# The last pair of down projections of a block moves behind the next block's output projection

## The chip, the cores and the metric

The kernel runs on one core of one Trainium2 chip. The metric is the device time of one execution in microseconds. The engines named below are TensorE (PE, with its weight loads as PEld), VectorE (DVE), ScalarE (ACT), GpSimd (POOL) and SyncE (SP, which issues the DMA transfers).

## The reference

One transformer layer on 2048 tokens of width 512. Attention has 32 heads of 16 with a single key and value head; the feed-forward part is a gated bilinear unit of width 1792. Shifts, scales and gates come from a condition vector.

```python
mod = (silu(c) @ w_mod).reshape(c.shape[0], 6, 1, -1)
sa, ca, ga, sb, cb, gb = (mod[:, i] for i in range(6))
h = layernorm(x) * (1 + ca) + sa
q = (h @ wq)             # 32 heads of 16
k, v = h @ wk, h @ wv    # one head of 16
p = softmax((q @ k.T) * 16 ** -0.5)
x = x + ga * ((p @ v) @ wo)
h = layernorm(x) * (1 + cb) + sb
x = x + gb * (((h @ w_gate) * (h @ w_up)) @ w_down)
```

## The kernel before, in words

The 2048 tokens are cut into 4 blocks of 512. Attention of a block is 8 **units** of 4 heads each, so there are 32 units, 0 to 31; a unit is 32 **steps**, and the loop has 1024 of them. A step computes, two times over, 512 columns of scores for the running maximum of the next unit (tile `mx`, reduced by DVE into `mpart`), 512 columns of scores (tile `sc`, exponentiated by ACT into tile `P`) and 512 columns of the product with the values (tile `pv`). So a step has two exponentials on ACT and two maximum reductions on DVE.

All other matmuls are **fill**: the planner puts them between these, at the end of a step. Fill consists of groups, each the sum over a long contraction into one PSUM bank (tile `misc`; the bank is `misc` or `spare`): the query projections (16 groups of 12 terms, in units 0 to 7), and then for each block the output projection (`wo_work`, 4 groups of 12), the gate and up projections (`ffn_work`, 28 groups of 12) and the down projections (4 groups of 42). Operands are split into high and low halves in fp16, which gives three terms per product.

A term of a group is computed as two **halves**, one on the upper 64 rows of PE and one on the lower 64. Two groups run side by side: one on rows 0 to 63, the other on rows 64 to 127; together that is a **pair** of halves, eight PE instructions of 64x32 by 512 columns. A group starts on the upper half beside the lower half of its predecessor, which is called the carry. A stretch of such pairs that ends with an eviction is a **turn** (`begin_turn`, `end_turn`); a turn of gate or up groups has 12 pairs. The first group of a chain has no predecessor and the last no successor, so at both ends 12 halves run alone. Down projections come as `twos`: two groups that take 12, 30 and 42 pairs.

The queue `fill` is in an order written out by hand at step 16 of the first unit of a block: the 4 output projections of the block just finished, the transposes of the second normalisation (`ln2_work`, "solo" items, four, one for each 128 columns), the 28 gate and up groups, the two pairs of down projections. Each item has a due step. `pace` works out from the due steps how many pairs a step has to take, and `fill_gap` issues up to `BURST` = 3 pairs per step from the credit so gained. A turn starts `EV_WAIT` = 1 step after one that ended with an eviction, else `SWAP_WAIT` = 2. The transposes wait `TR_GAP` = 8 steps after the output projection, for its sums (`x1`), their statistics on DVE and POOL and the normalised rows `n2` on ACT. A transposed piece goes through ACT (`hf`, two buffers) and is split by POOL into the two halves of `h2T`. While block 0 is treated, POOL also still splits the feed-forward weights (tile `wsl` into `wg` and `wu`), one slice every two or three steps, in an order that does not depend on the fill.

The sums `x1` of a block live from its output projection to the end of its down projections, in a ring of 4 buffers that `hi` and `gab` of the start share. Block 3 has no attention after it: its work, and what is left of block 2, runs in a tail of plain 128x128 matmuls. The two pairs of down projections of block 2 are left to that tail.

Of the kernel before, what the change touches and what calls it, by code (L numbers as in the profile page):

```python
# [13 lines left out]
F32 = mybir.dt.float32  # L14
F16 = mybir.dt.float16
# [4 lines left out]
S, D, H, DH, F = 2048, 512, 32, 16, 1792  # L20
KC = D // 128
NB = 4
BT = S // NB
# [15 lines left out]
SWAP_WAIT = 2  # L39
EV_WAIT = 1  # L40
TURN = 12
RESERVE = 31000.0
TR_GAP = 8
BURST = 3
# [11 lines left out]
def adaln_mqa_glu_kernel(ctx: ExitStack, tc: tile.TileContext, x_in, wq_in, wk_in, wv_in, wo_in,  # L56
# [7 lines left out]
    work = ctx.enter_context(tc.tile_pool(name="work", bufs=2))  # L64
# [23 lines left out]
    def ps_misc(shape=(128, 512), dt=F32, tag=None):  # L88
        bufs = 1
        if tag is None:  # L90
            tag, bufs = ring["tags"][ring["n"] % len(ring["tags"])]
            ring["n"] += 1
        elif tag == "sc":
            bufs = NSC
        return psum.tile(list(shape), dt, name="misc", tag=tag, bufs=bufs)
# [102 lines left out]
    def rstd_of(st, n):  # L198
        y = work.tile([128, 4], F32, name="ry", bufs=6)[:, :n]
        rstd_into(y, st[:, :, 1], n)  # L200
        return y
# [59 lines left out]
                             start=(k == 0), stop=(k == KC - 1))  # L261

    def split_rows(dst, p, scale, mscale, bias):
        hi = work.tile([128, BT], F16, name="hi", tag="x1", bufs=4)
        nc.scalar.activation(hi, p, AF.Identity, bias=bias, scale=mscale)
        nc.vector.scalar_tensor_tensor(dst, p, scale, hi, op0=OP.mult, op1=OP.subtract)

# [396 lines left out]
    def after(delay, f):  # L664
        if tick[0] is None:
            f()
        else:
            timers.setdefault(tick[0] + delay, []).append(f)
# [6 lines left out]
    def load_x(b, t):  # L675
        xl = work.tile([128, D], F32, name="xl", tag="xl", bufs=3)
        r0 = b * BT + t * 128
        nc.sync.dma_start(xl, x_rows[r0:r0 + 128, :])
        xls[b, t] = xl

    def wo_work(b):
        def op(t):
            def f(i):
                ch, term = divmod(i, 3)
                ol, wl = TERMS[term]
                return och[b, ch][:, ol, t * 128:(t + 1) * 128], wo[:, wl, ch, :]
            return f

        def pre(t):
            def f(tag=None):  # L690
                load_x(b, t)
                return ps_misc(tag=tag)
            return f

        def fin(t):
            def f(p):
                if b < NB - 1:
                    x1 = work.tile([128, D], F32, name="x1", tag="x1", bufs=4)
                else:
                    x1 = work.tile([128, D], F32, name="x1p", tag="P", bufs=NP)  # L700
                nc.vector.scalar_tensor_tensor(x1, p, sca[:, 7:8], xls[b, t], op0=OP.mult, op1=OP.add)
                x1s[b, t] = x1
                s2 = work.tile([128, 1, 2], F32, name="st2", bufs=5)
                bs = work.tile([128, 6], F32, name="bs", bufs=4)
                nb = work.tile([128, 2], F32, name="nb", bufs=4)
                yt = {}

                def spread():
                    nc.vector.bn_stats(bs, x1)

                def aggr():
                    nc.vector.bn_aggr(s2[:, 0, :], bs)
                    yt["y"] = rstd_of(s2, 1)
                    nc.gpsimd.tensor_tensor(nb[:, 0:1], s2[:, 0, 0:1], yt["y"], op=OP.mult)
                    nc.gpsimd.tensor_scalar(nb[:, 1:2], nb[:, 0:1], -1.0, 0.0, op0=OP.mult, op1=OP.add)

                def nrm():
                    n2 = work.tile([128, D], F32, name="n2", tag="och", bufs=4)
                    nc.scalar.activation(n2, x1, AF.Identity, bias=nb[:, 1:2], scale=yt["y"])
                    n2s[b, t] = n2  # L720

                after(2, spread)
                after(3 + t % 2, aggr)
                n2f[b, t] = nrm
                if t == 3:
                    for j, d in enumerate((2, 3, 5, 7)):
                        after(d, n2f[b, j])
            return f

        return [Group(3 * KC, op(t), pre(t), fin(t)) for t in range(4)]  # L730
# [107 lines left out]
    def late_weights():  # L838
# [19 lines left out]
            nc.sync.dma_start(md, st["row"][64:128:32, :])  # L858
            st["md"] = md

        gab = work.tile([128, D], F32, name="gab", tag="x1", bufs=4)
        gbb = consts.tile([128, D], F32, name="gbb")

        def m3():
# [185 lines left out]
    fill = deque()  # L1050
    cur = {"gen": None, "segs": None, "stages": deque(), "carry": None, "j": 0, "wait": 0, "swap": False}
    credit = [0.0]

    def seg_left():
        n = sum(2 * x.g.n - x.k for x in live())
        return n / 2.0

    def live():
        xs = []
        for segs in ([cur["segs"]] if cur["segs"] else []) + [q[0] for q in cur["stages"]]:  # L1060
            xs += [x[0] for x in segs if x]
        xs += [cur["carry"]] if cur["carry"] else []
        return list({id(x): x for x in xs}.values())

    def pace(step):
# [4 lines left out]
        for _, kind, what, due in fill:  # L1070
            n += 4.0 if kind == "solo" else sum(g.n for g in what)
            kept = RESERVE / PAIR if due > (NB * UB - 1) * NSTEP else 0.0
            most = max(most, (n - kept) / max((due - step) / 2, 1.0))
# [15 lines left out]
    def begin_turn(segs, wait):  # L1089
        cur.update(segs=segs, j=0, wait=max(cur["wait"], wait))  # L1090

    def plan(step):
# [7 lines left out]
        if fill and fill[0][1] == "prod" and open_gate(step):  # L1100
# [12 lines left out]
            if carry:  # L1113
                begin_turn(((d1, 0, TURN), seg_u), cur["end"] + (EV_WAIT if cur["evicted"] else SWAP_WAIT))
                cur["stages"].append((((d1, TURN, n), (d2, 0, n - TURN)), EV_WAIT))
            else:
                begin_turn(((d1, 0, n), (d2, 0, n - TURN)), step)
            cur["stages"].append((((d2, 0, n), (d1, 0, n)), SWAP_WAIT))
            d2.u = n - TURN
            cur["carry"] = d2  # L1120
# [13 lines left out]
    def fill_gap(step):  # L1134
        if cur["segs"] is None and not plan(step):
            return
        if step < cur["wait"]:
            return
        n = min(int(credit[0]), BURST)
        late = -(-seg_left() // max(NU * NSTEP - 8 - step, 1))  # L1140
        burst_turn(step, max(1, n, int(late)))

# [77 lines left out]
    def ffn_twos(b):  # L1220
        gu, down = ffn_work(b)
        return [(g,) for two in gu for g in two] + twos(down)

    early["on"] = False
    for u in range(NU):
        b, g = divmod(u, UB)
        if u == 1:
            side.extend(dlist)
        for i in range(NSTEP):
            step = u * NSTEP + i  # L1230
            kt, p = divmod(i, 2)
            drain_posts()
            spare["scores"] = not spare["held"] and not (fill and fill[0][1] == "prod" and open_gate(step))
            a = p
            if p == 1:
                who = (u, kt - 1, 0) if kt else (u - 1, KT - 1, 0)
                if u and not kt:
                    posts.append(lambda u=u: pv_lower(u - 1))
            else:
                who = (u, kt - 2, 1) if kt > 1 else (u - 1, KT - 2 + kt, 1)  # L1240
                if u and kt == 1:
                    posts.append(lambda u=u: pv_out(u - 1))
            max_half(a, 0, 2)
            pv(*who, 0)
            qk_exp(u, kt, 0, a)
            max_half(a, 1, 2)
            pv(*who, 1)
            drain_mids()
            qk_exp(u, kt, 1, a)
            if p == 1:  # L1250
                late_max()
            if fill or live():
                credit[0] = min(credit[0] + pace(step) / 2, 6.0)
                if credit[0] >= 1.0:
                    fill_gap(step)
            side_step(step)
            if u > 0 and g % 2 == 0 and i in (5, 9, 15):
                if i == 5:
                    nrm = normalise((u - 1) // UB, ((u - 1) % UB) // 2)
                nrm[(5, 9, 15).index(i)]()  # L1260
            if i == 16 and u > 0 and g == 0:
                ln = ln2_work(b - 1)
                due = (b + 1) * UB * NSTEP + (DUE if b < NB - 1 else LAST_DUE)
                gate = [step + 4, 0]
                for gr in wo_work(b - 1):
                    fill.append((gate, "prod", (gr,), due))
                for gap, it in zip((TR_GAP, 0, 0, 0), ln):
                    fill.append(([None, gap], "solo", it, due))
                gate = [None, 0]
                for gs in ffn_twos(b - 1):  # L1270
                    fill.append((gate, "prod", gs, due))

    def drain_all():
# [66 lines left out]
```

## Time and profile before

| | us |
|---|---|
| median of 3 runs | 1734.06 |
| lowest and highest | 1729.01, 1734.56 |
| the profiled execution | 1740.9 |
| its span, first to last instruction | 1739.1 |
| attention loop with fill, within the span | about 92 to 1574 |
| the tail's plain matmuls, last long stretch | 1610.44 to 1735.21 |

The profiled execution is slower than the median; differences are worked out within it and then set against the median. PE is busy for 97% of the span, but a busy PE is not PE at its peak, since matmuls are pipelined. In a view of windows, each row has the stretch, its length, and for each engine the busy time and in brackets the number of instructions, then the granted TensorE clock, the share of the DMA engines and GB/s. A window that is filtered to one line or one tile shows the engines that have such instructions.

### The profile page before, as it was taken

How to read it: one execution, taken by the hardware profiler on the slowest of the kernel's cores; microseconds unless marked ns; L12 is line 12 of the kernel's file. 1: busy time of each engine (PE TensorE's matmuls, PEld its weight loads, DVE VectorE, ACT ScalarE, POOL GpSimd, SP SyncE). 2: the span in 40 equal slices, each digit the busy share in tenths (PEclk: the TensorE clock that was granted, in tenths of full speed). 3: DMA queues.
4: the chain of work that ended last, by engine and by line, in shares of the span. 5: the costliest groups of instructions: out<-in, count | busy, mean ns of one | idle time of the engine just before them, and what ended most of it. 6: DMA issues, size and time to landing. Idle time of an engine off the chain costs nothing. (4 is left out here: it accounts for less than half of the span.)

```text
span 1739.1 us, 102797 instructions
## 1 busy us (share of the span) xinstructions
PE 1686.9 (97%) x47395; PEld 972.1 (56%) x47395; DVE 1406.3 (81%) x2353; ACT 1253.0 (72%) x2319; POOL 560.1 (32%) x745
## 2 busy tenths in 40 slices
PE   6899999999999999999999999999999999999999
PEld 3345555544546566566556666666556666654444
DVE  7899999999987888888898888888999999912110
ACT  3479898989876787777787777777788888883110
POOL 5824444637575842210022212210021222221130
PEclk9999999999998999999999999999999999999999
DMA  5212232312322210000100000000100000001000
GB/s 198 102 33 82 63 88 62 93 40 86 84 70 58 66 28 17 7 17 25 43 24 19 13 19 13 8 19 21 49 17 19 12 19 13 15 7 46 15 1 25
DMA packets 49180, 71.10 MB, mean 41 GB/s; under 512 B 15270, under 2 KB 29418, under 8 KB 48748
## 3 DMA queue, kind: packets, MB, share of 16 engines
q1 hardware_dynamic: 47164, 64.33, 12.3%
q8 instruction: 370, 6.06, 1.5%
q14 instruction: 62, 0.51, 0.1%
q10 hardware_dynamic: 1584, 0.20, 0.1%
HBM read 51.12 MB, written 8.92 MB: 35 GB/s over the span
## 5 line engine op out<-in xcount | busy, mean ns | idle before, releaser
L564 DVE TENSOR_REDUCE mpart<-mx 128x1 f32<-128x512 f32 x2048 | 1290.8, 683 | 125.1 <-PE mx L487 110.5
L600 ACT ACTIVATE P<-sc 128x512 f32<-128x512 f32 x2048 | 1128.4, 599 | 279.6 <-PE sc L487 235.9
L612 PE MATMUL pv<-P,vst 64*32 64x256 f32 x16384 | 1172.3, 383 | 0.3 <-issue 0.3
L487 PE MATMUL mx<-kst,sst 48*32 48x512 f16 x8192 | 819.8, 382 | 25.9 <-DVE mpart L564 19.2
L487 PE MATMUL sc<-sst,kst 50*32 50x512 f16 x8192 | 828.8, 379 | 2.3 <-ACT P L600 2.0
L487 PEld LDWEIGHTS <-sst 48*32 48x32 f16 x8192 | 333.2, 91 | 355.7 <-issue 243.0
L612 PEld LDWEIGHTS pv<-P,vst 64*32 64x32 f32 x16384 | 418.2, 105 | 56.5 <-issue 5.3
L487 PEld LDWEIGHTS <-kst 50*32 50x32 f16 x8192 | 303.3, 91 | 75.7 <-issue 32.8
L487 PE MATMUL misc<-h2T,wg 64*32 64x512 f16 x4032 | 307.1, 379 | 0.3
L487 PE MATMUL misc<-h2T,wu 64*32 64x512 f16 x4032 | 305.1, 376 | 0.7 <-issue 0.2
L795 POOL TENSOR_TENSOR gf<-gf,g 128x512 f32<-128x512 f32 x42 | 53.9, 1282 | 470.8 <-ACT gf L794 470.6
L487 PEld LDWEIGHTS <-wu 64*32 64x32 f16 x4032 | 111.1, 92 | 40.1 <-issue 12.9
L487 PEld LDWEIGHTS <-wg 64*32 64x32 f16 x4032 | 112.4, 93 | 37.8 <-issue 13.5
L487 PE MATMUL misc<-wd,glu 64*32 64x512 f16 x2688 | 114.1, 376 | 0.1
L787 ACT ACTIVATE g<-misc 128x512 f32<-128x512 f32 x56 | 33.6, 601 | 75.8 <-PE misc L520 75.5
L652 POOL TENSOR_TENSOR oc<-oc,rr 128x512 f32<-128x512 f32 x15 | 19.3, 1285 | 213.7 <-DMA rr<-ri 186.2
L487 PE MATMUL misc<-h,wq 64*32 64x512 f16 x1536 | 85.0, 378 | 0.6
L520 PE MATMUL misc<-wd,glu 128*128 128x512 f16 x336 | 73.2, 379 | 0.0
L487 PEld LDWEIGHTS <-glu 64*32 64x32 f16 x2688 | 53.1, 93 | 26.1 <-issue 6.0
L799 POOL TENSOR_TENSOR glu<-gf,glu 128x512 f16<-128x512 f32 x56 | 65.1, 1163 | 4.7
L797 DVE TENSOR_TENSOR gf<-misc,g 128x512 f32<-128x512 f32 x14 | 9.7, 692 | 62.9 <-PE misc L520 62.9
L625 DVE SCALAR_TENSOR_TENSOR ev<-pv,evs,ev 128x512 f32<-128x512 f32 x32 | 23.8, 743 | 45.1 <-ACT ev L620 36.4
(231 smaller groups left out, 1037.3 us busy)
## 6 DMA issues: line engine op xcount, KB each, us to landing
wsl<-in_B_w_gate_dram SPq DMA_DIRECT2D x32, 224.0 KB
wsl<-in_B_w_up_dram SPq DMA_DIRECT2D x32, 224.0 KB
wsl<-in_B_w_down_dram SPq DMA_DIRECT2D x28, 256.0 KB
sst<-qd SPq DMA_DIRECT2D x186, 32.0 KB
qd<-q SPq DMA_DIRECT2D x16, 256.0 KB
oc<-ev SPq DMA_DIRECT2D x128, 32.0 KB
rr<-ri SPq DMA_DIRECT2D x16, 256.0 KB
xl<-in_A_x_dram SPq DMA_DIRECT2D x16, 256.0 KB
```

Source lines behind the costliest of these rows:

```text
L487: return [nc.tensor.matmul(p[c:c + CW, :], left[:, c:c + CW], right, start=start, stop=stop) for c in range(0, 128, CW)]
L520: nc.tensor.matmul(p, left, right, start=i == 0, stop=i == g.n - 1)
L564: nc.vector.tensor_reduce(mparts[u][:, a, p, t, kc:kc + 1], m, axis=AX.X, op=OP.max)
L600: nc.scalar.activation(ptl[u, kt, a][:, p, :], t, AF.Exp)
L612: nc.tensor.matmul(pvb[u, r][32 * j:32 * j + 32, c * w:(c + 1) * w], vst[ks, kt, :], ptl[u, kt, a][ks, p, c * w:(c + 1) * w], start=(kt == ...
L625: nc.vector.scalar_tensor_tensor(ev, pvb[u, 1], evs, ev, op0=OP.mult, op1=OP.add)
L652: eng.tensor_tensor(o, o, st["r"], op=OP.mult)
L787: nc.scalar.activation(st["g", f], p, AF.Copy, scale=2.0 ** -45)
L795: nc.gpsimd.tensor_tensor(gf, gf, st["g", f], op=OP.mult)
L797: nc.vector.tensor_tensor(gf, p, st["g", f], op=OP.mult)
L799: nc.gpsimd.tensor_tensor(st["glu"][:, 1, f, :], gf, st["glu"][:, 0, f, :], op=OP.subtract)
```

## The change

Three edits. The ring of `x1` gets 6 buffers. When the work of block 0 or block 1 is queued, its last two down projections are taken off the list and kept (`held`); they are queued 8 units later, behind the next block's output projections, with a due step 44 steps on (`HELD_DUE`), and the wait of 8 steps before the transposes is then 0. And in `fill_gap`, where a burst would leave exactly one pair of a turn, it takes one pair more, or, where it is at 3 already, one less.

```diff
+NX1 = 6
+HELD_DUE = 44
...
-        hi = work.tile([128, BT], F16, name="hi", tag="x1", bufs=4)
+        hi = work.tile([128, BT], F16, name="hi", tag="x1", bufs=NX1)
...
-                    x1 = work.tile([128, D], F32, name="x1", tag="x1", bufs=4)
+                    x1 = work.tile([128, D], F32, name="x1", tag="x1", bufs=NX1)
...
         n = min(int(credit[0]), BURST)
+        left = max(x[2] - x[1] for x in cur["segs"] if x) - cur["j"]
+        if left - n == 1:
+            n += 1 if n < BURST else -1
         late = -(-seg_left() // max(NU * NSTEP - 8 - step, 1))
...
+    held = []
     for u in range(NU):
...
                 for gr in wo_work(b - 1):
                     fill.append((gate, "prod", (gr,), due))
-                for gap, it in zip((TR_GAP, 0, 0, 0), ln):
+                for gs in held:
+                    fill.append((gate, "prod", gs, step + HELD_DUE))
+                for gap, it in zip((0 if held else TR_GAP, 0, 0, 0), ln):
                     fill.append(([None, gap], "solo", it, due))
                 gate = [None, 0]
-                for gs in ffn_twos(b - 1):
+                work_items = ffn_twos(b - 1)
+                held = [work_items.pop()] if b < NB - 1 else []
+                for gs in work_items:
                     fill.append((gate, "prod", gs, due))
```

How many pairs each unit gets, counted in the order of the two programs:

| unit | 8 | 9 | 10 | 11 | 12 | 13 | 14 | 15 | 16 | 17 | 18 | 19 | 20 | 21 | 22 | 23 | 24 | 25 | 26 | 27 | 28 | 29 | 30 | 31 |
|---|---|---|---|---|---|---|---|---|---|---|---|---|---|---|---|---|---|---|---|---|---|---|---|---|
| before | 31 | 41 | 81 | 77 | 78 | 76 | 79 | 77 | 67 | 41 | 81 | 77 | 78 | 76 | 79 | 77 | 65 | 34 | 66 | 61 | 62 | 60 | 62 | 34 |
| after | 29 | 41 | 66 | 65 | 66 | 65 | 64 | 66 | 63 | 93 | 64 | 71 | 71 | 70 | 71 | 71 | 65 | 93 | 61 | 66 | 67 | 67 | 66 | 39 |

A halved pair at a chain's end counts as one here. The order shows the move on ACT at the second hand-over (units 16 to 18: block 1's output projection, then its transposes). `n` are the normalised rows, `hf` the transposed pieces, each `P` an exponential. Before, from the third normalised row on:

```order
L719 ACTIVATE n_27581<-x_27190,nb,ry 128x512
L600 ACTIVATE P<-sc 128x512 x4
L719 ACTIVATE n_27649<-x_27421,nb,ry 128x512
L600 ACTIVATE P<-sc 128x512 x6
L751 ACTIVATE hf<-misc,hsc 128x512
L600 ACTIVATE P<-sc 128x512 x2
```

After:

```order
L721 ACTIVATE n_26911<-x_26413,nb,ry 128x512
L602 ACTIVATE P<-sc 128x512 x4
L721 ACTIVATE n_27027<-x_26660,nb,ry 128x512
L602 ACTIVATE P<-sc 128x512 x26
L583 ACTIVATE mt_27757<-mxt 16x128
L602 ACTIVATE P<-sc 128x512 x12
L622 ACTIVATE ev<-pv,evs 128x512
L602 ACTIVATE P<-sc 128x512 x12
L753 ACTIVATE hf<-misc,hsc 128x512
L602 ACTIVATE P<-sc 128x512 x2
```

Three steps (6 exponentials) lay between the last normalised row and the first transposed piece; now it is 25 (50 exponentials), and the held pair of down projections runs in them.

On DVE the same place shows that pair's two results. After the change, from the statistics of block 1's last output projection:

```order
L714 BN_AGGR st_26662<-bs 128x2
L566 TENSOR_REDUCE mpart<-mx 128x1 x28
L572 TENSOR_REDUCE mm<-mpart 128x16
L566 TENSOR_REDUCE mpart<-mx 128x1 x4
L584 SCALAR_TENSOR_TENSOR mt_27758<-mxt,mt_27757 16x128
L566 TENSOR_REDUCE mpart<-mx 128x1 x12
L814 SCALAR_TENSOR_TENSOR x_13696<-misc,sca,x_13696 128x512
```

`x_13696` is a sum of block 0; before, its row stood ahead of block 1's four output projections.

The third place is POOL at the first hand-over (unit 9, where nothing is held). `wsl` is a slice of the feed-forward weights, `h2T` the transposed pieces. Before:

```order
L753 TENSOR_SCALAR h2T<-hf 128x512
L754 TENSOR_TENSOR h2T<-hf,h2T 128x512
L976 TENSOR_SCALAR wsl<-wsl,sca 128x448
L977 TENSOR_SCALAR wg<-wsl 128x448
L978 TENSOR_TENSOR wg<-wsl,wg 128x448
L753 TENSOR_SCALAR h2T<-hf 128x512
L754 TENSOR_TENSOR h2T<-hf,h2T 128x512
L753 TENSOR_SCALAR h2T<-hf 128x512
L754 TENSOR_TENSOR h2T<-hf,h2T 128x512
L753 TENSOR_SCALAR h2T<-hf 128x512
L754 TENSOR_TENSOR h2T<-hf,h2T 128x512
```

After:

```order
L980 TENSOR_TENSOR wg<-wsl,wg 128x448
L755 TENSOR_SCALAR h2T<-hf 128x512
L756 TENSOR_TENSOR h2T<-hf,h2T 128x512
L755 TENSOR_SCALAR h2T<-hf 128x512
L756 TENSOR_TENSOR h2T<-hf,h2T 128x512
L755 TENSOR_SCALAR h2T<-hf 128x512
L756 TENSOR_TENSOR h2T<-hf,h2T 128x512
L978 TENSOR_SCALAR wsl<-wsl,sca 128x448
L979 TENSOR_SCALAR wg<-wsl 128x448
L980 TENSOR_TENSOR wg<-wsl,wg 128x448
L755 TENSOR_SCALAR h2T<-hf 128x512
L756 TENSOR_TENSOR h2T<-hf,h2T 128x512
```

The weight slice that stood between the first and the second conversion stands ahead of the first, and the next one between the third and the fourth.

More of the change, by code (lines that the diff above doesn't have):

```diff
@@ L859, in m2 @@
             st["md"] = md
-        gab = work.tile([128, D], F32, name="gab", tag="x1", bufs=4)
+        gab = work.tile([128, D], F32, name="gab", tag="x1", bufs=NX1)
         gbb = consts.tile([128, D], F32, name="gbb")
```

## The prediction

> **What bounds the kernel now.** The page first: who is busy, and what ends last.
>
> ```profile
> span 1739.1 us, 102797 instructions
> PE 1686.9 (97%) x47395; PEld 972.1 (56%) x47395; DVE 1406.3 (81%) x2353; ACT 1253.0 (72%) x2319; POOL 560.1 (32%) x745
> PE misc L520 8%; PE misc L744 0%; DVE x1p L812 0%; DVE och L655 0%; DVE oc L652 0%; DVE och L654 0%
> ```
>
> The chain of waits holds only the tail (8%, plain matmuls of L520 back to back), which the change leaves with the same work. The time must be read from the attention loop. Its clock is the exponential of L600: two per step, so a window that holds 2n of them is n steps (an odd one more is the neighbour's). Windows of L600 alone:
>
> ```profile
> 1071.24:1116.44 45.20, 32.69 (x61) 1.00 0.05 13
> 988.10:1063.20 75.10, 54.65 (x101) 1.00 0.06 13
> 1365.95:1382.84 16.89, 13.07 (x25) 1.00 0.06 13
> 1203.14:1214.77 11.63, 7.97 (x16) 1.00 0.02 5
> 815.71:827.03 11.32, 8.03 (x16) 1.00 0.02 5
> 1237.95:1242.72 4.77, 3.96 (x8) 1.00 0.37 101
> 533.70:825.50 291.80, 210.32 (x386) 1.00 0.11 30
> 922.66:1213.05 290.39, 210.45 (x386) 1.00 0.07 17
> 1309.16:1535.44 226.28, 175.03 (x320) 1.00 0.06 15
> ```
>
> The same windows for instructions on tile misc, the accumulators of the fill; eight PE instructions are one pair of halves (unit 17, 874.18 to 922.66, is added; some PE records are missing, so counts run a little low):
>
> ```profile
> 1071.24:1116.44 45.20, 22.15 (x578) 0.00 (x0) 0.00 (x0) 3.62 (x6) 1.00 0.05 13
> 988.10:1063.20 75.10, 38.31 (x971) 0.00 (x0) 0.00 (x0) 6.00 (x10) 1.00 0.06 13
> 1365.95:1382.84 16.89, 8.04 (x200) 0.00 (x0) 0.00 (x0) 1.21 (x2) 1.00 0.06 13
> 1203.14:1214.77 11.63, 6.10 (x168) 0.00 (x0) 0.00 (x0) 0.00 (x0) 1.00 0.02 5
> 815.71:827.03 11.32, 5.65 (x168) 0.00 (x0) 0.00 (x0) 0.00 (x0) 1.00 0.02 5
> 1237.95:1242.72 4.77, 0.00 (x0) 0.00 (x0) 0.00 (x0) 0.00 (x0) 1.00 0.37 101
> 874.18:922.66 48.48, 15.06 (x256) 1.68 (x16) 2.23 (x3) 3.35 (x4) 1.00 0.04 11
> 533.70:825.50 291.80, 149.76 (x3744) 0.00 (x0) 1.48 (x2) 16.84 (x28) 1.00 0.11 30
> 1261.52:1309.16 47.64, 13.25 (x228) 1.67 (x16) 2.23 (x3) 3.34 (x4) 1.00 0.06 16
> ```
>
> That gives a price list. No fill: 4 steps in 4.77, 1.19 us a step. Two pairs: 12 steps, 24 pairs, 1.407. Five-step turns at 2.4 pairs: 50 steps and 120 pairs in 75.10, 1.502. Three pairs: 7 steps each, 21 pairs, 1.661 and 1.617; I take the dearer. From 2.0 to 2.4 one pair a step more costs 0.24 us, from 2.4 to 3 0.27; between none and two it costs 0.11. So a pair is cheap where a step is empty and dear where it is full.
>
> **The change part by part.** I counted pairs per unit (32 steps) in the order of both programs. All pairs, all single halves (168 in each) and the work left to the tail are equal in number; only places change.
>
> *Part 1, block 0's stretch (units 10 to 15).* Its last two down projections leave it: 468 pairs (3744/8) become 392, 2.04 a step. 192 steps at 1.407+0.04x0.24=1.417 are 272.1; the window stood 1.6 above its own price (192x1.512=290.2 against 291.80), which I keep. 273.7 against 291.8: **-18.1**.
>
> *Part 2, units 17 and 25, where the held pair goes.* Before, about half of their steps are empty or hold only transposes. Now each holds 93 pairs: 31 steps of three and one empty. 31x1.661+1.2=52.7. Beside it lie the next block's output projections, whose sums and statistics go to DVE. Two rows of DVE's timeline in unit 17, then the four steps of that unit with transposes (window of L600), and the seven after them (window of misc):
>
> ```profile
> 895.24 0.75 DVE L701 SCALAR_TENSOR_TENSOR x<-misc,sca,xl 128x512 f32<-128x512 f32 x1 [0.19 <-PE misc L487]
> 897.10 0.68 DVE L709 BATCH_NORM_STATS2 bs<-x 128x6 f32<-128x512 f32 x1
> 905.71:912.42 6.71, 5.22 (x11) 1.00 0.01 2
> 912.42:922.66 10.24, 3.55 (x49) 0.00 (x0) 0.00 (x0) 0.82 (x1) 1.00 0.02 5
> ```
>
> Four steps at DVE's own rate are 4x1.19, with 0.75+0.68 together 6.2 us, under four full steps of 6.64: hidden. If that cover fails it costs up to 1.43 for each of three projections, 4.3; I take 1. 53.7 against 48.48 and 47.64: **+5.2 and +6.1**. The eight-step wait before the transposes falls away; the held pair covers the normalisation.
>
> *Part 3, units 18 and 26, into which the transposes slip.* Unit 18 now holds: 2 full steps 3.3; eight steps of single halves (the window from 912.42 has four, with three nearly empty steps, in 10.24: about 1.62 each) 13.0; four steps with transposes (the window of L600 from 905.71) 6.7; four empty steps 5.0; 14 steps at 2.43 pairs 21.1. Sum 49.1. Units 19 to 23 have 354 pairs in 160 steps, 2.21, 1.457 a step: 233.2. Together 282.3 against 290.39: **-8.1**. Unit 26 alike, with 3 pairs fewer, 48.4; units 27 to 30 go up to 266 pairs in 128 steps, 1.426: 182.5. 230.9 against 226.28: **+4.6**. Units 16, 24 and 31 change by few pairs: **+0.5** together.
>
> *Part 4, block 0's hand-over (unit 9).* Nothing is held there, but the new turn rule shifts the fill by one step, and the order of POOL with it. Before, ACT, POOL and PE, and windows of all engines (last columns: granted clock, DMA):
>
> ```profile
> 513.43 0.64 POOL L976 TENSOR_SCALAR wsl<-wsl,sca 128x448 f32<-128x448 f32 x1
> ...
> 516.51 1.16 POOL L754 TENSOR_TENSOR h2T<-hf,h2T 128x512 f16<-128x512 f32 x1
> 517.70 0.78 ACT L751 ACTIVATE hf<-misc,hsc 128x512 f32<-128x512 f32 x1 [1.95 <-POOL h2T L754]
> 519.02 0.62 PE L487 MATMUL sc<-sst,kst 50*32 50x512 f16 x4 [1.75 <-ACT P L600]
> 515.00:520.00 5.00, 3.13 (x72) 1.72 (x76) 2.62 (x5) 2.83 (x6) 4.83 (x6) 0.87 0.17 49
> 520.00:525.00 5.00, 5.00 (x89) 2.24 (x74) 2.55 (x5) 2.22 (x5) 4.66 (x7) 0.50 0.00 1
> 525.00:530.00 5.00, 5.00 (x80) 2.63 (x80) 2.58 (x4) 2.39 (x4) 3.76 (x5) 0.50 0.45 116
> 530.00:535.00 5.00, 5.00 (x117) 2.72 (x111) 3.61 (x6) 2.84 (x6) 4.61 (x7) 0.76 0.09 31
> 515.41:533.70 18.29, 6.08 (x49) 0.00 (x0) 0.00 (x0) 0.78 (x1) 0.63 0.19 53
> ```
>
> A weight split (513.43, three instructions) stands between the first and second h2T conversion. The fourth hf waits 1.95 us for its buffer, the exponentials queue behind it, PE stops 1.75 us, and the granted clock is 0.50 until about 532.4 (13.7 us, from the four rows). The seven steps take 18.29 us where the same seven of unit 17, with the same 49 PE instructions on misc, take 10.24. In the changed order the split stands ahead of the first conversion and the next one only behind the third, and the fourth hf comes a step later: its buffer is free. **-8.1**; between 0 (the wait returns) and 8.1 no row argues for a middle.
>
> The Trainium skill, TensorE: Matmul & The Clock Gate, Part 1, says that one busy window of some 3.4 us releases the clock. This trace does not agree: busy PE stayed at 0.50 for 13.7 us. By that page the stall would be worth some 1.95+1.7=3.7 (an estimate from it), and my sum 4.4 less.
>
> *Part 5, the turn rule.* 1071.24 to 1116.44 has only turns that end on one pair, 988.10 to 1063.20 only turns that don't: 45.20/30=1.507 and 75.10/50=1.502 a step, both at 2.4 pairs. So the single pair at the end costs next to nothing. The rule pushes it to the next turn's head: 26 turns now begin with one pair, in the step in which ACT has an eviction (0.60, so 1.21/2 in the window from 1365.95) beside two exponentials. Unused PE room there is at most one pair, 0.24; at the least nothing. Near the lower end, because ACT's queue may lag: 26x0.08=**+2**. In the query projections:
>
> ```profile
> 136.55:346.74 210.19, 179.36 (x321) 1.00 0.26 76
> L701 DVE SCALAR_TENSOR_TENSOR x<-misc,sca,xl 128x512 f32<-128x512 f32 x12 | 8.9, 745 | 0.6 <-PE misc L487 0.4
> ```
>
> these 160 steps run at 1.314 with less than one pair each; twelve times, two single pairs become a two and an empty step: 12x(1.407+1.19-2x1.314) is -0.4; I take **+0.5**, for bounds of -0.4 and +1.5.
>
> *At nothing:* the two x1 buffers (SBUF only). On SP the held tiles' two stores go behind the next block's four x loads instead of ahead; L701 waited 0.6 us in all for its inputs, and those loads still have eight steps. POOL has no work in a down projection.
>
> **Sum:** -18.1+5.2+6.1-8.1+4.6+0.5-8.1+2+0.5 = -15.4. The profiled execution took 1740.9 (span 1739.1); 6.8 above the median of 1734.06, a plain offset that I carry: 1734.06-15.4 = 1718.7, said as **1718**.
>
> **Rivals.**
> *A. A pair has one price everywhere.* Then moving pairs is neutral, and only the floor in empty steps counts. Take 0.98+0.216 a pair: unit 17 stood 48.48-40.2=8.3 above that, after 53.7-51.5=2.2; unit 18 goes from about 0 to 3.9 above. 2 gained per hand-over, 4 in two, 8.1 from part 4, less 2.5 of part 5: 9.6, **1724**. For it: 2.4 to 3 pairs costs what 2.0 to 2.4 does. Against: 0.11 a pair below two. The Trainium skill, same page, Back-to-back issue gap, gives about 216 ns per matmul of 512 columns, which is this rival's price.
> *B. Part 4 fails:* the fourth hf waits again and the clock drops. The forecast without it: **1726**.
> *C. Full units get an engine as bound.* If x1 sums, statistics and evictions on DVE stretch the 62 full steps from 1.661 to 1.9, that is 15: **1733**, no change; it decides from 0.16 a step on (10 us). Against it: the 6.2 under 6.64 above.
> *D. Slower: the stall comes from transposes as such.* They now follow single halves with no gap. If each set stops PE for 1.75 us and drops the clock, units 18 and 26 lose 8.1 each and part 4 gains nothing: -7.3+16.2, **1743**. One stall alone leaves a gain; from two and an uncured unit 9 on it is slower. Against it: 905.71 to 912.42 has such a set at clock 1.00 with no splits on POOL.
>
> **How the numbers follow.** Forecast 0.58, A 0.17, B 0.13, C 0.07, D 0.05. A measurement tells about 0.3% (5.2 us): faster is under 1728.9. Faster: forecast, A and most of B (0.09), 0.84; same: the rest of B and most of C, 0.10; slower 0.06. Range: below, part 5 free (2.5), the x1 sums free (2), full steps at 1.617 (62x0.044=2.7) and the 1.6 of part 1 gone, 1709; above, B with its 8.1 and the x1 sums at their upper end for one unit (4.3 for 1), 1729. It holds A and B and leaves out C and D, 0.12, and some of the edges.
>
> **What would show it.** Units 10 to 15 near 274 us; units 17 and 25 at 53 to 55 with 93 pairs each; no clock of 0.50 between the start-up and the end; the fourth hf without a wait; about 1.41 in turns of two pairs, not 1.45, also with one pair at the head. Wrong would be: full units over 58, or a stop of PE at the transposes of units 18 and 26.

## The result and the profile after

| | us |
|---|---|
| changed kernel, median of 4 runs | 1720.93 (1719.64 to 1721.67) |
| before, median of 4 runs beside it | 1734.31 (1729.01 to 1736.91) |
| ratio, with its 95% interval | 0.992 (0.9895 to 0.9946) |
| the same two again in a later group of runs (7 and 17) | 0.9938 (0.9914 to 0.9963) |

The change is worth 13.4 us in the first comparison and 10.6 in the second; 1718 was forecast, 15.4 (said as 16) below the 1734.06 of before. First the page of the changed kernel:

```profile
span 1719.9 us, 102799 instructions
PE 1667.0 (97%) x47395; PEld 987.9 (57%) x47395; DVE 1408.3 (82%) x2353; ACT 1256.3 (73%) x2319; POOL 558.9 (32%) x745
PE misc L522 8%; PE misc L746 0%; DVE x1p L814 0%; DVE och L657 0%; DVE oc L654 0%; DVE och L656 0%
```

The same number of matmuls and the same chain, so all of it must lie in the loop. The span is 19.2 us shorter, while the medians are 13.4 apart: a first sign that something in the profiled execution of before is not in the median. The loop in windows of the exponentials (L602 now), each from the first score of a unit to that of another: units 10 to 15, 17, 18 to 23, 25, 26 to 30:

```profile
527.18:801.71 274.53, 209.57 (x385) 1.00 0.11 31
849.25:900.74 51.49, 35.06 (x65) 1.00 0.05 12
900.74:1184.99 284.25, 210.20 (x385) 1.00 0.06 17
1233.34:1285.02 51.68, 35.05 (x65) 1.00 0.04 11
1285.02:1516.53 231.51, 174.82 (x320) 1.00 0.07 17
```

The same windows of tile misc, where eight PE instructions are a pair:

```profile
527.18:801.71 274.53, 129.49 (x3132) 0.00 (x0) 0.00 (x0) 16.81 (x28) 1.00 0.11 31
849.25:900.74 51.49, 27.28 (x752) 0.00 (x0) 2.25 (x3) 0.00 (x0) 1.00 0.05 12
900.74:1184.99 284.25, 135.31 (x3268) 1.68 (x16) 1.50 (x2) 19.97 (x32) 1.00 0.06 17
1233.34:1285.02 51.68, 27.30 (x748) 0.00 (x0) 2.25 (x3) 0.00 (x0) 1.00 0.04 11
1285.02:1516.53 231.51, 108.91 (x2548) 1.68 (x16) 1.50 (x2) 17.48 (x28) 1.00 0.07 17
```

The 3744 instructions of units 10 to 15 have become 3132, and unit 17 went from 256 to 752 in 3.0 us more. The hand-over of block 0 (unit 9) on ACT, on POOL and in windows of all engines:

```profile
513.46 0.86 ACT L753 ACTIVATE hf<-misc,hsc 128x512 f32<-128x512 f32 x1
515.08 0.89 ACT L753 ACTIVATE hf<-misc,hsc 128x512 f32<-128x512 f32 x1
516.80 0.81 ACT L753 ACTIVATE hf<-misc,hsc 128x512 f32<-128x512 f32 x1
519.76 0.78 ACT L753 ACTIVATE hf<-misc,hsc 128x512 f32<-128x512 f32 x1
```

```profile
516.94 1.16 POOL L756 TENSOR_TENSOR h2T<-hf,h2T 128x512 f16<-128x512 f32 x1
518.07 0.62 POOL L755 TENSOR_SCALAR h2T<-hf 128x512 f16<-128x512 f32 x1
```

```profile
515.00:520.00 5.00, 4.89 (x121) 2.62 (x128) 3.99 (x7) 4.99 (x10) 4.75 (x7) 1.00 0.16 49
520.00:525.00 5.00, 4.57 (x138) 2.69 (x125) 4.21 (x8) 3.92 (x8) 4.67 (x7) 1.00 0.17 46
```

No hf has a wait in brackets. The buffer that the fourth one (519.76) needs is read last by the second conversion, which ends at 518.10. PE goes on, and the granted clock stays at 1.00. Unit 9 takes 48.55 us (478.63 to 527.18), 56.52 before.

### The profile page after: what moved, and what is told of

Read it like the earlier page. It is cut to its first block, busy times and chain, and to the rows that moved or that the text cites. A ratio compares the mean times of both kernels' runs of the same rounds, so it can differ in the third digit from the quotient of the medians.

```text
span 1719.9 us, 102799 instructions
## 1 busy us (share of the span) xinstructions
PE 1667.0 (97%) x47395; PEld 987.9 (57%) x47395; DVE 1408.3 (82%) x2353; ACT 1256.3 (73%) x2319; POOL 558.9 (32%) x745
## 5 line engine op out<-in xcount | busy, mean ns | idle before, releaser
L602 ACT ACTIVATE P<-sc 128x512 f32<-128x512 f32 x2048 | 1126.9, 598 | 257.5 <-PE sc L489 211.9
L614 PEld LDWEIGHTS pv<-P,vst 64*32 64x32 f32 x16384 | 415.4, 105 | 53.7 <-issue 3.3
L489 PEld LDWEIGHTS <-kst 50*32 50x32 f16 x8192 | 306.8, 90 | 64.4 <-issue 27.1
L489 PEld LDWEIGHTS <-wg 64*32 64x32 f16 x4032 | 114.9, 92 | 36.9 <-issue 12.8
L489 PE MATMUL misc<-wd,glu 64*32 64x512 f16 x2688 | 119.1, 376 | 0.7 <-issue 0.5
L654 POOL TENSOR_TENSOR oc<-oc,rr 128x512 f32<-128x512 f32 x15 | 19.2, 1279 | 144.9 <-DMA rr<-ri 55.5
L627 DVE SCALAR_TENSOR_TENSOR ev<-pv,evs,ev 128x512 f32<-128x512 f32 x32 | 23.8, 743 | 44.7 <-ACT ev L622 36.5
```

Source lines behind the costliest of these rows:

```text
L489: return [nc.tensor.matmul(p[c:c + CW, :], left[:, c:c + CW], right, start=start, stop=stop) for c in range(0, 128, CW)]
L602: nc.scalar.activation(ptl[u, kt, a][:, p, :], t, AF.Exp)
L614: nc.tensor.matmul(pvb[u, r][32 * j:32 * j + 32, c * w:(c + 1) * w], vst[ks, kt, :], ptl[u, kt, a][ks, p, c * w:(c + 1) * w], start=(kt == ...
L627: nc.vector.scalar_tensor_tensor(ev, pvb[u, 1], evs, ev, op0=OP.mult, op1=OP.add)
L654: eng.tensor_tensor(o, o, st["r"], op=OP.mult)
```

## The experiments

The theory under test is that of the prediction: pairs are cheap where a step is empty and dear where it is full, unit 9's stall is worth 8.1, and the turn rule costs a little. The rival explanations are one price for every pair, and that all of the gain is the cured stall. Ratios are against the kernel before in the same group of runs (medians of before 1737.47, 1739.37 and 1736.25 in the three groups). Expected times were reckoned from 1734.06 for the kernel before, so a measurement is set against them by its ratio.

### The two halves of the change, and the stall alone

*e1: the held pair without the turn rule (from the changed kernel).*

```diff
-        left = max(x[2] - x[1] for x in cur["segs"] if x) - cur["j"]
-        if left - n == 1:
-            n += 1 if n < BURST else -1
```

> Only the held pair (with its six x1 buffers), without the rule on the last pair of a turn. By the price list the rule is worth -2 to +2 us, so this is the changed kernel again: 1719 to 1723 us, unit 17 at 51 to 53 us, units 10 to 15 at 273 to 276 us. In unit 9 the fill also shifts by a step here, so the stall and the half clock should be absent. Rival (the single pairs were the cost): 1727 us or more.

Measured: 1727.19, ratio 0.9943 (0.9927 to 0.9958). As ratios the expected times are 0.991 to 0.994 and the rival's 0.996 or more: the interval takes in the upper end of the first and ends just short of the second. In the profile units 9 and 17 take 47.8 and 51.1 us, as expected, and units 10 to 15 278.9, where 273 to 276 was expected. The six buffers of `x1` were not run by themselves.

*e2: the turn rule without the held pair (the three lines added to the kernel before).*

> Only the rule on the last pair of a turn; nothing held. By the price list: units 10 to 31 as before within 3 us, unit 9 about 8 us shorter because the order of POOL changes there, so 1725 to 1729 us. Rival (the single pairs were the cost): 1721 us or less. Rival (the stall in unit 9 is rare outside of profiles): 1732 us or more.

Measured: 1731.75, ratio 0.9968 (0.995 to 0.9986), at the upper end of the 0.995 to 0.997 that the expected times mean.

*e3: neither of them; in the kernel before, one more step ahead of block 0's transposes, which moves them past the weight slice on POOL.*

```diff
-                for gap, it in zip((TR_GAP, 0, 0, 0), ln):
+                for gap, it in zip((TR_GAP + (b == 1), 0, 0, 0), ln):
```

> The kernel before, with the wait ahead of block 0's transposes 9 steps instead of 8; nothing else. It moves one weight slice on POOL ahead of the first conversion. If the stall of unit 9 is worth its 8 us in every execution: 1725 to 1728 us, no clock of 0.50 inside the loop, unit 9 near 49 us. If the half clock comes only in some executions, or costs little by itself: 1730 to 1733 us. If the stall hangs on the transposes as such: 1734 us.

Measured: 1730.99, ratio 0.9968 (0.9955 to 0.9981). That lies between the expectations for the whole 8 us (0.9948 to 0.9965) and for less of it (0.9977 to 0.9994), and the interval reaches both. Its unit 9 has the clock at 1.00 throughout (48.15 us), as has that of e2 (48.62).

e2 and e3 have the same ratio, and in their profiles units 10 to 31 take 1035.9 and 1036.2 us: the turn rule by itself gives nothing but the shift that cures the stall. The held pair gives more than that, 0.9943 or less against 0.9968: each of the six runs of e1 (1728.57 at most) lies under each of the eleven of e3 (1728.83 at least), so the gain isn't all the cured stall. Beside the held pair the rule is worth 1 to 4 us by the runs (0.9943 against 0.992 and 0.9938), with intervals that overlap. The profiles point the same way in units 10 to 15, with 278.9 us in e1 against 274.5 and 272.4 with the rule. This is left open, but the rule isn't slower.

### The stall put back, and cured in another way

*e5: the changed kernel once more, for a second profile and as the neighbour of e6.*

> The changed kernel itself, on the chip of the next three, as their yardstick: 13 to 14 us under the kernel before, ratio 0.992. If the rule on the last pair of a turn is worth nothing beside the held pair, this ratio is that of the held pair alone (0.9943) within its interval.

Measured: 1728.79 (1716.34 to 1729.65, the lowest being the profiled execution), ratio 0.9938 (0.9914 to 0.9963). That is 10.6 us under the kernel before, less than the 13 to 14 expected, and it agrees with the 0.9943 of e1 within the interval. Units 10 to 15 and 18 to 23 in its profile:

```profile
527.16:799.58 272.42, 209.85 (x386) 1.00 0.12 32
898.77:1179.53 280.76, 210.07 (x385) 1.00 0.07 17
```

2.1 and 3.5 us less than in the first profile of the same program. That is how far one profile can be read.

*e6: the changed kernel with block 0's transposes one step earlier, so that POOL again has a weight slice between the first two conversions. A transpose of block 0 also takes less of the credit, so that the four come in four steps in a row.*

```diff
-            credit[0] -= 4.0
+            credit[0] -= 4.0 if step > 320 else 2.5
...
-                for gap, it in zip((0 if held else TR_GAP, 0, 0, 0), ln):
+                for gap, it in zip((0 if held else TR_GAP - 1, 0, 0, 0), ln):
```

> The changed kernel with block 0's transposes one step earlier and in four steps in a row, so that POOL again has a weight slice between the first and the second conversion. If the stall is what unit 9 gained: the fourth hf waits about 2 us, a clock of 0.50 inside the loop, and 5 to 8 us slower than the changed kernel. If the wait alone counts and the half clock doesn't come: 2 us slower. If unit 9 gained by something else: no slower.

The stall is back: the fourth hf on ACT, then windows of all engines with the granted clock third from the end:

```profile
519.72 0.78 ACT L753 ACTIVATE hf<-misc,hsc 128x512 f32<-128x512 f32 x1 [1.94 <-POOL h2T L756]
```

```profile
520.00:525.00 5.00, 4.45 (x84) 2.71 (x87) 2.08 (x3) 2.67 (x5) 4.67 (x7) 0.65 0.01 1
525.00:530.00 5.00, 5.00 (x77) 2.18 (x73) 2.36 (x4) 2.54 (x5) 4.67 (x7) 0.50 0.19 52
530.00:535.00 5.00, 5.00 (x100) 3.28 (x92) 2.77 (x4) 2.39 (x4) 4.56 (x7) 0.50 0.28 92
```

Unit 9 takes 57.80 us in this profile, 9.2 more than in e5's; it holds 49 pairs instead of 41, so a little of that is fill. Yet the median is 1728.49, ratio 0.9942 (0.9919 to 0.9965), against 0.9938 for e5. The mechanism is as predicted in the profile, and its price is not found in the runs. The profiled execution (1731.22) is the slowest of the six and has a mean granted clock of 0.992; the other five have 0.995 to 0.997, which is at most some 17 us at half clock in all. The start-up of this profile has 13.7 of that by itself, so none of the five has room for another 13.7 in unit 9.

*e7: the kernel before with a third buffer for hf (and for the other tiles of its ring); the order stays.*

```diff
...
-                hf = work.tile([128, BT], F32, name="hf", tag="g", bufs=2)
+                hf = work.tile([128, BT], F32, name="hf", tag="g", bufs=3)
...
```

> The kernel before with three buffers instead of two for hf (and the gate sums, which share them); the order of every engine stays. The fourth hf then has a free buffer although POOL is as late as before. If the wait for the buffer starts the stall: no wait of ACT there, no clock of 0.50, 5 to 8 us under the kernel before, ratio 0.995 to 0.997. If POOL's lateness itself stops PE: ratio 0.999 to 1.001.

The fourth hf no longer waits, and the clock holds:

```profile
520.41 0.81 ACT L751 ACTIVATE hf<-misc,hsc 128x512 f32<-128x512 f32 x1
```

```profile
520.00:525.00 5.00, 4.89 (x128) 2.20 (x130) 4.23 (x9) 4.63 (x10) 4.75 (x7) 1.00 0.19 49
```

Unit 9 takes 48.39 us, so the wait comes from the missing buffer, by POOL's order. The runs: 1736.01, ratio 0.9988 (0.9974 to 1.0002), at most 4.5 us. The time misses the expected 0.995 to 0.997 and fits the rival's 0.999 to 1.001, though the profile rules that rival out: POOL's order is the old one and PE doesn't stop. A part of the answer may lie in the start-up, whose tiles share the ring. The mean clock of this profile is 0.993 with no stall in it, since more of the start-up ran at half clock than before. All engines, first of e7, then of before (the granted clock is third from the end):

```profile
84.00:106.00 22.00, 20.44 (x269) 8.35 (x269) 16.18 (x28) 7.30 (x14) 8.98 (x9) 0.61 0.29 87
```

```profile
80.00:102.00 22.00, 20.17 (x305) 7.84 (x305) 17.85 (x31) 8.59 (x17) 10.34 (x10) 0.77 0.34 95
```

Seven of e7's twelve runs have 0.993 or 0.994, the other five 0.996; yet those five have a median of 1736.14, so the start-up doesn't explain it all. The 2.1 us between the ratios is not a clean price of the stall.

### What a pair costs in each place

In e9 and e10 the last two down projections of blocks 0 and 1 sum 18 of their 42 terms; the other 24 are left out, in the old place and in the new one. That takes 48 pairs out of each hand-over (2 groups of 24 terms of 2 halves).

```diff
-        return gu, [Group(3 * FT, dn(t), ps_misc, fin(t)) for t in range(4)]
+        return gu, [Group(18 if b < 2 and t > 1 else 3 * FT, dn(t), ps_misc, fin(t)) for t in range(4)]
```

*e9: in the kernel before.*

> The kernel before, in which the last two down projections of blocks 0 and 1 sum 18 of their 42 terms only, so 96 pairs of halves are left out, in the place where they stood: units 10 to 16 and 18 to 24 at 2.4 pairs a step. By the price list 96 x 0.24 = 23 us less than the kernel before, ratio 0.987. With a fixed price of 0.216: 21 us. If a pair there is mostly hidden: under 12 us.

Measured: 1717.7, ratio 0.9894 (0.9879 to 0.991), 18.5 less than before and less than either price said (23 and 21). Fewer pairs also shift unit 9, and its stall is gone (48.69 us), so the comparison is with e3. Units 10 to 15 and 18 to 23 of e3, then of e9, tile misc:

```profile
528.06:817.92 289.86, 147.40 (x3748) 0.00 (x0) 1.49 (x2) 16.88 (x28) 1.00 0.12 32
914.73:1204.31 289.58, 147.41 (x3744) 0.00 (x0) 1.49 (x2) 16.86 (x28) 1.00 0.06 17
```

```profile
526.23:808.15 281.92, 134.38 (x3388) 0.00 (x0) 1.49 (x2) 16.92 (x28) 1.00 0.12 31
904.72:1185.80 281.08, 135.23 (x3388) 0.00 (x0) 1.48 (x2) 16.93 (x28) 1.00 0.06 16
```

45 pairs less are 7.9 and 8.5 us less: 0.18 and 0.19 a pair. The evictions on ACT are 28 in all four rows, so this is the price of the pairs and not of evictions left out with them; units 10 to 15 have 103 steps with three pairs in e3 and 57 in e9, so it is mostly the third pair of a step that went. By the runs it is less, since e3 has 5.6 of the 18.5: 12.9 for 96 pairs, 0.13. Units 26 to 30 of e9, with as many pairs as before, took 230.61 against 225.29 in e3, which is the rest.

*e10: in the changed kernel; the held pair's due step and the gap behind it keep the transposes where they are.*

```diff
-HELD_DUE = 44
+HELD_DUE = 28
...
-                for gap, it in zip((0 if held else TR_GAP, 0, 0, 0), ln):
+                for gap, it in zip((16 if held else TR_GAP, 0, 0, 0), ln):
```

> The changed kernel with the same 96 pairs left out of the held groups, and 16 steps of waiting put in their place, so that everything else stands in the same step: in units 17 and 25 sixteen steps of three pairs become empty. By the price list 2 x 16 x (1.661 - 1.19) = 15 us less than the changed kernel, so some 27 us under the kernel before, ratio 0.984. If a pair costs the same in the new place as in the old: 23 us less than the changed kernel, 35 under the kernel before, ratio 0.980.

Measured: 1713.81, ratio 0.9874 (0.9856 to 0.9893): less was saved than by either expectation (0.984 and 0.980). Units 17 and 18 of the changed kernel, then of e10, tile misc (unit 17 of the first stands above):

```profile
900.74:950.63 49.89, 21.84 (x440) 1.68 (x16) 1.50 (x2) 4.31 (x6) 1.00 0.09 27
```

```profile
848.43:897.75 49.32, 18.44 (x464) 0.00 (x0) 3.75 (x5) 0.00 (x0) 1.00 0.08 22
897.75:944.04 46.29, 16.10 (x336) 1.68 (x16) 0.00 (x0) 4.34 (x6) 1.00 0.07 17
```

101.38 us with 1192 instructions against 95.61 with 800: 49 pairs for 5.8 us, 0.12 a pair (0.09 with e5's 100.12). By the runs, 0.9874 against 0.992 and 0.9938 is 8 to 11 us for 96 pairs, 0.08 to 0.12. A pair is cheaper behind the output projection (0.09 to 0.12 by the profiles) than where it stood (0.18 and 0.19). By the runs alone it is 0.08 to 0.12 against 0.13, and there the intervals overlap. All of these lie under the forecasts for e9 and e10, 0.24 and 0.16. In e10 empty steps and full ones stand near each other, five of each; the full ones have two normalised rows on ACT beside them (exponentials, then tile misc):

```profile
894.16:900.14 5.98, 5.51 (x10) 1.00 0.02 4
869.98:877.52 7.54, 5.29 (x11) 1.00 0.03 8
```

```profile
894.16:900.14 5.98, 0.00 (x0) 0.00 (x0) 0.00 (x0) 0.00 (x0) 1.00 0.02 4
869.98:877.52 7.54, 4.32 (x128) 0.00 (x0) 0.00 (x0) 0.00 (x0) 1.00 0.03 8
```

1.20 us a step with no fill and 1.51 with three pairs (the 128 counted instructions are a little more than 15 pairs): 0.10 a pair.

### A later due step

Units 10 to 15 still hold two pairs a step, while units 16 and 24 have eight empty steps at a chain's end. A later due step for all items of a block (DUE) takes pairs out of the first and fills the second.

```diff
-DUE = 12
+DUE = 24
```

*e4: the changed kernel with DUE at 24.*

> The changed kernel, with each block's fill due at step 24 of the second unit after it instead of step 12, so that the first down pair runs into the next output projection without a break: 24 single halves fewer at each of two hand-overs and some 14 empty steps filled. By the price list: 24 pairs' worth of steps less at 0.24 us, 5.8 us, and some 28 pairs that cost 0.11 us instead of 0.24, 3.6 us: 1710 to 1714 us. Rival (single halves and empty steps cost nothing that the rest doesn't take back): 1719 to 1722 us.

Measured: 1716.93 (1711.05 to 1718.1), ratio 0.9876 (0.9857 to 0.9895), inside the 0.986 to 0.988 that the expected times mean; the rival's 0.991 to 0.993 lies outside the interval.

*e8: that, and RESERVE, a constant that paces the last units, from 31000 to 33500.*

> The changed kernel with due step 24 instead of 12 between blocks, and with 33500 instead of 31000 ns of work kept for the tail, which spreads the last block's fill over 4 more steps of its end: 64 pairs per unit in units 27 to 30, all of them in twos, instead of 66 or 67. By the price list 12 pairs go from 0.24 to 0.11 us, 1.5 us, beside the first edit's 7 to 9: 8 to 11 us under the changed kernel, ratio to before 0.986 to 0.988. Rival (the first edit alone counts): ratio 0.988.

Measured: 1716.43, ratio 0.9877 (0.9852 to 0.9901): RESERVE adds nothing that shows.

*e11: as e8 with DUE at 22. At 24 the chain of gate, up and down projections runs on into the next output projection and one chain end per hand-over falls away (120 single halves in the whole program instead of 168); at 22 the end stays.*

> Due step 22 instead of 24 with 33500 ns kept for the tail: the first down pair still ends just before the next output projection starts, so at units 16 and 24 the empty steps are filled, but the 24 single halves at each hand-over stay. By the price list 24 single halves stand in the place of 12 pairs, 12 x 0.24 = 2.9 us for each hand-over: 5 to 6 us over the kernel with due step 24, ratio to before 0.990 to 0.992. Rival (empty steps are all that step 24 saves): the same as with 24.

Measured: 1719.38, ratio 0.99 (0.9884 to 0.9916), as expected.

*e12: e8 again, beside e11.*

> Due step 24 with 33500 ns kept, on the chip of the other three: ratio to before 0.986 to 0.989, 5 to 6 us under due step 22.

Measured: 1713.41, ratio 0.9871 (0.9847 to 0.9895). Units 10 to 15 and unit 16 of e12, tile misc:

```profile
526.77:797.63 270.86, 124.34 (x2956) 0.00 (x0) 0.00 (x0) 16.83 (x28) 1.00 0.12 32
797.63:847.48 49.85, 24.48 (x624) 0.00 (x0) 2.24 (x3) 0.00 (x0) 1.00 0.17 49
```

22 pairs fewer than in the changed kernel take 3.7 us off the first window; unit 16 has 78 pairs instead of 63 and costs 2.3 more. The medians of e11 and e12 are 6.0 apart, as forecast for the chain ends, but their intervals just overlap; it points to the single halves and doesn't settle it. The traces point there too: steps that hold three single halves, with no eviction and no hand-over of a unit, average 1.57 us (eight steps in units 17 and 25 of before) and 1.51 (seven in units 18 to 23 of the changed kernel), nearly the 1.58 of three whole pairs. DUE at 24 is the best version that ran with all of the layer's terms: 0.9871 to 0.9877 in three groups of runs against 0.992 and 0.9938, which is 7 to 12 us under the changed kernel.

## Why the prediction was right, point by point

1720.93 lies in the range of 1709 to 1729, halfway between the forecast's 1718 and rival A's 1724, so the time alone doesn't tell these two apart. The moved pairs do: without the stall the forecast has 7.3 for them and the turn rule, rival A 1.5, and the runs give 5 to 8 (0.992 and 0.9938 against the 0.9968 of e2 and e3, where only the stall is cured). B, C and D have their places below. The upper end of the range is 1730.1 by its own terms (1718.7+8.1+3.3) instead of 1729, which changes nothing here. The measured parts, in us of the first profile and of e5's, against that of before:

| part | predicted | first | e5 |
|---|---|---|---|
| 1: units 10 to 15 | -18.1 | -17.3 | -19.4 |
| 2: units 17, 25 | +5.2, +6.1 | +3.0, +4.0 | +3.1, +3.6 |
| 3: units 18 to 23 | -8.1 | -6.1 | -9.6 |
| 3: units 26 to 30 | +4.6 | +5.2 | +6.0 |
| 3: units 16, 24, 31 | +0.5 | -0.9 | -1.0 |
| 4: unit 9 | -8.1 | -8.0 | -8.0 |
| 5: turn rule, beside the units | +2 | in the units | in the units |
| 5: units 0 to 7 | +0.5 | +1.8 | +1.8 |

**Part 1 held.** 274.53 and 272.42 against 273.7. The price came out right for this kind of stretch, where the fill is turns of gate and up groups, each with an eviction on ACT.

**Part 2: the price of a full step was a little too high, and the cover was thinner than said.** The term was 31 steps at 1.661. The row it came from holds the step in which a unit's maxima are handed to the next one. Its first two steps and its next four, exponentials of before:

```profile
1203.14:1206.91 3.77, 2.90 (x6) 1.00 0.02 4
1206.91:1213.05 6.14, 4.05 (x8) 1.00 0.02 4
```

The first two take 1.89 each, with ACT, PE and DVE passing the maxima (mxt, mt) in them; the four plain ones 1.535. In the changed kernel's unit 17 the first 12 steps, beside the output projection's sums, statistics and normalised rows, and the next 7, beside little:

```profile
849.25:869.61 20.36, 13.32 (x25) 1.00 0.09 21
869.61:880.18 10.57, 7.48 (x15) 1.00 0.02 5
```

1.70 and 1.51 a step. So the work of the output projections, of which three steps in twelve carry a sum and three a statistic, isn't hidden there: 12 x 0.19 = 2.2 where 1 was taken, inside its bounds of 0 and 4.3. Not all of it need be theirs, since a unit's own eviction of the attention product (L622 on ACT, L627 on DVE) lies in the twelve steps too.

These are single short rows. All steps of a trace can be sorted instead: a step lasts from its first score matmul to that of the next step, and its pairs are the matmuls on misc over eight. The table has the mean time in us, with the number of steps in brackets. Steps at the hand-over of a unit, where its maxima or its attention product are passed on, are left out. In the first three columns neither ACT nor DVE reads misc; in the last one of them does, which is an eviction of fill.

| steps with | 1 pair | 2 pairs | 3 pairs | 3 pairs and an eviction |
|---|---|---|---|---|
| before, units 10 to 15 | 1.29 (12) | 1.39 (57) | 1.56 (71) | 1.81 (20) |
| e3, units 10 to 15 | 1.23 (13) | 1.32 (60) | 1.60 (62) | 1.79 (21) |
| changed, units 10 to 15 | 1.29 (2) | 1.37 (125) | 1.60 (13) | 1.78 (3) |
| changed, units 17 and 25 | none | none | 1.58 (48) | 1.69 (4, sums on DVE) |

All 62 full steps of units 17 and 25 together average 1.62, with the hand-over and the sums in them. 31 x 1.62 + 1.2 = 51.4, and 51.5 and 51.7 were measured instead of 53.7: the term's 1.661 was 0.04 too dear, and the 1 for the sums was counted on top of it. Rival C's 1.9 a step is not there.

So the forecast's sentence "a pair is cheap where a step is empty and dear where it is full" holds, near the numbers of its list (0.11 a pair up to two, 0.24 to 0.27 beyond). The second pair of a step costs about 0.1, the third 0.17 to 0.28, and an eviction in a full step some 0.2 more. From an empty step (1.20 in e10) to three pairs it is 0.38, or 0.13 a pair. A full step costs the same in the old place as in the new one. The old place was dear because many of its pairs stood third in their step, and the new one is cheap because it had empty steps to fill; e9 and e10 fit this with their 0.18 and 0.12. Rival A's single price is not there. The change brings the steps of three pairs in units 10 to 15 from 104 down to 23, and those with an eviction from 23 to 3, hand-over steps included. That the evictions cost what the table says is read from sorted steps; no run moves evictions alone. The Trainium skill, TensorE: Matmul & The Clock Gate, Back-to-back issue gap, gives some 216 ns for a single matmul of 512 columns and 131 in a sustained stream; in these traces a pair has no one price, from about 0.1 to 0.28.

**Part 3 held in sum.** -1.8 and -4.6 in the two profiles around the -3.0 predicted, and PE does not stop at the transposes of units 18 and 26 (its longest wait in either unit is 0.6 us, and the clock stays at 1.00), which rules out D. Unit 18 took 49.89 and 48.59, for 49.1.

**Part 4: right in place and mechanism, too large in the runs.** The wait, the buffer and POOL's order were shown by e3, e6 and e7. But the step "6.8 above the median, a plain offset that I carry" failed: the profiled execution of before, at 1740.9 and a mean granted clock of 0.993, was one of the worst. In 46 later runs of that kernel the mean clock is 0.995 in 31 (median 1737.43), 0.996 or 0.997 in 10, 0.994 in 3 and 0.992 in only 2 (1742.06 and 1743.88, of the three slowest); e3, without the stall, has 0.996 in 8 of 11. A mean lower by 0.001 is 3.4 us at half clock (0.001 x 1720 / 0.5), worth 1.7. So in a typical run the clock loses far less at the stall than the 13.7 us at 0.50 that the profile shows. With the wait of 1.95 that is some 3.7 instead of 8.1, an estimate, since the means are rounded to 0.001; e3 measured 5.6 (3.3 to 7.8), e7 2.1 with a longer start-up, e6 none. Rival B, by which the wait returns, did not happen, but its 1726 was too far off for the same reason. The Trainium skill, same page, Part 1, releases the clock after one busy window of about 3.4 us; the profile of before disagrees with its 13.7, and the mean clock of most runs leaves room for about one such window. Which execution keeps the long stretch, and why, stays open.

**Part 5: no cost was found.** Two stretches of 18 steps and three evictions each, one in turns of 1, 2, 2, 2, 2 and 3 pairs and one in turns of twos:

```profile
672.20:696.96 24.76, 19.66 (x37) 1.00 0.07 17
719.37:744.00 24.63, 19.64 (x38) 1.00 0.09 25
```

0.04 us per turn, half of the 0.08 taken, and 1.38 and 1.37 a step where 1.41 was the sign to look for. Over 26 turns that is 1.1, and the comparisons of e2 with e3 and of e1 with the changed kernel show no loss. The 1.8 of units 0 to 7 is not the rule's either: unit 0 alone took 1.7 more, and the start-up's half clock lasted 3.4 us longer than in the profile of before.

**The sum.** The shortfall against 15.4 is 2 to 5 us in the runs. The term that was too large is part 4's: by the runs the stall gave 0 to 6 of its 8.1. In the profiles parts 2 and 5 came out some 6 cheaper than forecast; the runs show little of that. These errors have opposite signs, so that 1718 lies within 3 us of the first measurement is in part luck. Against the profile of e3, units 10 to 31 gain 7.5 us (the first profile) and 12.8 (e5), and the runs stand at the lower end of these.

## What to carry to other kernels

Take a marginal price from many steps, sorted by what else they hold: one hand-over inside a seven-step window gave 1.661 us for a full step, where 48 plain ones average 1.58. Where single profiles of one program differ by 5 us and its runs have different mean clocks, look at the clock of every run before a clock drop seen in one profile is counted at its full length. Ask how full a step is before work is moved into it: here the third pair of a step cost 0.17 to 0.28 us and the first two about 0.1 each or less, so work from full steps gained by going where steps were empty.

## What the runs showed of the hardware

In both profiles with the stall, where PE stopped for 1.75 us (before) and 2.02 us (e6), the granted clock fell to 0.50 and stayed there for 13.7 us, with PE busy behind the stop (windows of 5.00 busy in 5.00). In the timed runs of the same programs the mean clock leaves room for far less. Two profiles of the changed kernel differ by 5.4 us in span, 5.3 of them in units 10 to 31, with the order of every engine the same, and by 1.8 us in one unit (unit 30: 43.82 and 45.63).
